# First three weight pieces in buffers of their own, shared with the general path's pool, and some instructions pinned in program order

## The chip, the cores and the metric

One core of a Trainium2 chip. The time is the device time of one execution in microseconds (us). The engines are PE (TensorE), DVE (VectorE), ACT (ScalarE), POOL (GpSimd) and SP (SyncE, which here only issues DMA transfers and register work). Three runs of the kernel before gave 1166.86, 1168.65 and 1170.96 us; the median is 1168.65.

## The reference

Three stages, each feeding the next. All data are fp32.

```python
# attention: B, H, S, D = 4, 8, 768, 64; first 4 keys (sink) and a window of 128 keys are kept
scores = where(is_sink | in_window, q @ k.T / sqrt(D), -1e9)
a = softmax(scores);  x = a @ v            # -> x: 3072 tokens x 512
# feed-forward: w_in 512 x 2048, w_out 2048 x 512
h = maximum(x @ w_in, 0);  x = (h * h) @ w_out
# top-1 mixture: 8 experts, w1 512 x 1024, w2 1024 x 512
e = argmax(x @ w_gate);  g = softmax(x @ w_gate)[e] * sigmoid((x @ w_og)[e])
out = g * (maximum(x @ w1[e], 0) @ w2[e])
```

`n_sink` and `window` are inputs. The kernel handles the values 4 and 128 on its fast path and any other on a slow general path.

## The kernel before, in words

**Tiling.** The 3072 tokens are taken as 12 blocks of 256 (`t` = 0 to 11), each with four pairs of heads (`p` = 0 to 3) and two halves of 128 queries (`n`). For a block, attention gives `xT` (128 x 4 x 256); then 16 steps `l1(t, j)` (L565, with squaring at L569 and splitting at L571 and L572) and `l2(t, j)` (L581) do the feed-forward with j over 16 slices of 128 hidden units. Attention of block t+1 is woven into the feed-forward of block t. After block 11 the mixture's slots follow.

**Precision.** fp32 matrices are split into a high and a low part, and three matmuls replace one. So the weights must be split once, before block 0 can use them: `conv(c)`, c = 0 to 31, takes one piece of 512 KB. An even c is the slice of `w_in` that `l1(0, c/2)` needs (tile `WI`); an odd c is the slice of `w_out` for `l2` (tile `WOa` for the first eight, `WOb` for the others). A conversion is a load by SP (L273 or L277) into a buffer `craw`, two ACT instructions in place (L283, L284), two DVE `SCALAR_TENSOR_TENSOR` into `fbuf` (L286, L287), a copy to the high part (L289 on ACT, or L291 on DVE for every third c), and the low part by subtraction on POOL (L292). `fbuf` has two halves in turn. `craw` shares a ring of three buffers (tag `stage`) with the scratch tiles `tmp` of `setup` and `setup2`.

**The start.** `scalars` loads the two inputs and computes `gen`. Every engine reads `gen` into a register (`values_load`, L784) and branches on it (L785): the branch holds `general`, the slow path, which isn't taken here. The pool `genp` of the slow path takes its SBUF from where the pool `wpool2` with `WOb` lies after it. Behind the branch a loop over 46 half steps places attention of block 0 (and the first events of block 1), `setup2` and one `conv` every third half step (`cstep`); then `split_x(0)` (L528 to L532) makes the `xT` of block 0, and the main loop begins. In it `cstep` brings the other conversions while block 0's feed-forward runs.

```python
def cstep(n):
    ...
        while st_["load"] < min(NC, st_["done"] + 2):   # loads run two ahead
            rests[st_["load"]] = conv(st_["load"])
```

**What sets the order.** Outside the last stage the order on each engine isn't the program's: a scheduler orders instructions by priority and by its own costs, between branches, and it may lift an instruction ahead of a branch when nothing forbids it. `tc.keep_in_program_order(x)` takes that freedom from an instruction. Engines run their lists in order. `fill` (L86) issues matmuls on a constant tile `idle` that only keep PE busy. `loads(t, p)` brings k, q, v of a pair of heads (L314) into tiles `kn`, `qn`, `vn`, two buffers each. In attention, `scores` makes the masked scores on DVE (L425, two instructions with the read of the minimum), the exponent on ACT (L428) and the normalisation (L438 on DVE, L440 on ACT); `prep_k` adds four sink keys to `kT` on POOL (L336 to L340); `setup2` has many small POOL instructions, among them the memset L230, and two DVE casts (L243) that read what it wrote.

Of the kernel before, what the change touches and what calls it, by code (L numbers as in the profile page):

```python
# [8 lines left out]
F32 = mybir.dt.float32  # L9
F32R = mybir.dt.float32r  # L10
BF16 = mybir.dt.bfloat16
I32 = mybir.dt.int32
# [23 lines left out]

SPLITS = {6: (0, 0), 8: (2, 0), 11: (0, 1), 12: (1, 0), 13: (2, 1), 14: (3, 0)}
NSLOT = NT // 128 + NE - 1
PRE = 2
# [3 lines left out]
def kern(ctx, tc, q, k, v, n_sink, window, w_in, w_out, w_gate, w_og, w1, w2, out):  # L43
# [34 lines left out]
    two = const.tile([1, 2], I32, name="two")  # L78
    idle = const.tile([128, 512], BF16, name="idle")
    V.memset(idle[:], 1.0)  # L80

    def fill(o, n):

        w = o.shape[-1]
        for _ in range(n):
            PE.matmul(o, lhsT=idle[:, 0:128], rhs=idle[:, 0:w], start=True, stop=True)  # L86

# [96 lines left out]
    def setup():  # L184
# [19 lines left out]
        A.activation(out=zz, in_=zz, func=AF.Exp)  # L204

    def setup2():

# [25 lines left out]
        wg = [tmp[:, 256:384].rearrange("p (a k c) -> p a k c", a=2, k=4)[:, n] for n in range(2)]  # L233
        SY.dma_start(out=wg[0][:, :, 0:NE], in_=w_gate.rearrange("(k p) e -> p k e", p=128))
        SY.dma_start(out=wg[0][:, :, NE:2 * NE], in_=w_og.rearrange("(k p) e -> p k e", p=128))
        G.memset(w3[:], 0.0)
# [32 lines left out]
    def conv(c):  # L269
        j, which = divmod(c, 2)  # L270
        raw = cv.tile([128, 512, 2], I32, tag="stage", bufs=3, name="craw")
        if which == 0:
# [7 lines left out]
        def rest():  # L280
            L, Hh = raw[:, :, 0], raw[:, :, 1]

            A.activation(out=Hh.bitcast(F32), in_=Hh.bitcast(F32), func=AF.Copy, scale=2.0 ** -112)  # L283
            A.activation(out=L, in_=L.bitcast(U32), func=AF.Copy, scale=0.93 * 2.0 ** -29)  # L284
# [18 lines left out]
    def loads(t, p):  # L303
        b, u = divmod(t, NQ // 2)
        s0 = 256 * u
        for nm, src, m in (("k", k, 3), ("q", q, 2), ("v", v, 3)):
            x = att.tile([128, m, 2, D], F32, tag=nm + "n", name=nm + "n", bufs=2)
            lo = s0 - 128 * (m - 2)
            o = 0
            if lo < 0:  # L310
                lo, o = 0, 1
            nb = m - o
            for e in range(2):
                (A if nm == "q" and t == 0 and p < 2 else SY).dma_start(out=x[:, o:m, e, :],  # L314
                             in_=src[b, 2 * p + e, lo:lo + 128 * nb, :].rearrange("(n s) d -> s n d", s=128))
            nat[nm, t, p] = x
        if u == 0 and p == 0:
            x = att.tile([H * NS, D], F32, tag="vs", name="vs", bufs=1)
            SY.dma_start(out=x[:], in_=v[b, :, 0:NS, :])
            nat["vs", b] = x  # L320
# [446 lines left out]
    st_ = dict(load=0, done=0)  # L767

    def cstep(n):
        for _ in range(n):  # L770
            if st_["done"] >= NC:
                return
            while st_["load"] < min(NC, st_["done"] + 2):
                rests[st_["load"]] = conv(st_["load"])
                st_["load"] += 1
            rests.pop(st_["done"])()
            st_["done"] += 1
# [7 lines left out]
    with tc.If(gv > 0):  # L785
        with tc.tile_pool(name="genp", bufs=1) as gp_:
            general(gp_)
    wpool2 = ctx.enter_context(tc.tile_pool(name="wpool2", bufs=1))
    WO[1] = wpool2.tile([128, NF // 2, 2, 512], F32R, name="WOb")
    WOf[1] = WO[1][:].rearrange("p j a f -> p (j a f)")  # L790
    events = sorted((e for t in range(NBLK) for e in attn_events(t)), key=lambda e: e[0])
# [15 lines left out]
    for h in range(-46, 0):  # L807
        run_to(h)
        if h == -38:
            setup2()  # L810
        if h >= -39 and h % 3 == 0:
            cstep(1)
    split_x(0)

# [304 lines left out]
```

## Time and profile before

| | |
|---|---|
| median of three runs | 1168.65 us |
| profiled execution, its own time | 1168.36 us |
| its span | 1166.5 us |
| PE busy, matmuls | 1127.8 us (97%) |
| DVE busy | 739.7 us (63%) |
| ACT busy | 637.1 us (55%) |
| POOL busy | 468.5 us (40%) |

The span is what the trace covers; the 1.9 us beside it lie around it. A share of busy time is an average over stages with different limits, so the stretches are looked at one by one.

### The profile page before, as it was taken

The numbers are of one execution on the slowest core, as the hardware profiler recorded it, in microseconds if no ns is written. First come the engines' busy times: TensorE is split into PE (matmuls) and PEld (weight loads), VectorE is DVE, ScalarE is ACT, GpSimd is POOL, SyncE is SP. The second block draws the span as 40 slices with busy tenths as digits, with TensorE's granted clock in tenths as the row PEclk, the third lists the DMA queues.
The fourth block names the chain that finished last, engine by engine and source line by source line (L and its number), as shares of the span: only waits on it lengthen the run. The fifth ranks groups of instructions, "written<-read, shape, count | busy, mean of one in ns | idle before, by whom it ended". The sixth has DMA issues, their size and how long they took to land. (4 is left out here: it accounts for less than half of the span.)

```text
span 1166.5 us, 23899 instructions
## 1 busy us (share of the span) xinstructions
PE 1127.8 (97%) x7082; PEld 947.2 (81%) x7082; DVE 739.7 (63%) x2018; ACT 637.1 (55%) x1750; POOL 468.5 (40%) x949
## 2 busy tenths in 40 slices
PE   7898899999999999999999999999999999999996
PEld 3565688888888888888888888997788888888884
DVE  5889866667676667676667676557412566763153
ACT  5867676767676767676776766554232232232200
POOL 4466664336565326565335655220211122221111
PEclk9989899999999999999999999999999999999998
DMA  5656411111211121111211110296411456653110
GB/s 134 185 171 187 110 28 45 38 46 38 55 30 46 30 55 37 46 42 29 52 37 47 35 48 2 28 252 156 127 38 46 152 182 215 218 201 132 46 45 23
DMA packets 139388, 100.08 MB, mean 86 GB/s; under 512 B 103904, under 2 KB 112224, under 8 KB 139235
## 3 DMA queue, kind: packets, MB, share of 16 engines
q1 hardware_dynamic: 132674, 83.85, 26.1%
q0 software_dynamic: 5472, 14.19, 3.7%
q8 instruction: 64, 1.05, 0.4%
q14 instruction: 90, 0.73, 0.2%
q10 hardware_dynamic: 1088, 0.26, 0.1%
HBM read 85.56 MB, written 13.76 MB: 85 GB/s over the span
## 5 line engine op out<-in xcount | busy, mean ns | idle before, releaser
L565 PE MATMUL psh<-xT,WI 128*128 128x256 f32 x2304 | 314.0, 284 | 11.4 <-POOL WI L292 6.3
L565 PEld LDWEIGHTS psh<-xT,WI 128*128 128x128 f32 x2304 | 294.1, 189 | 29.9 <-POOL WI L292 8.8
L887 PE MATMUL psh<-WI,xt 128*128 (+1 forms) x672 | 165.1, 399 | 1.0 <-ACT xt L867 0.7
L569 DVE TENSOR_TENSOR r<-r 128x256 f32<-128x256 f32 x184 | 86.3, 470 | 118.1 <-ACT r L568 117.3
L581 PE MATMUL psx<-WOa,h 128*128 128x512 f32 x576 | 159.8, 410 | 0.6 <-DVE h L572 0.6
L581 PE MATMUL psx<-WOb,h 128*128 128x512 f32 x576 | 157.2, 409 | 1.8 <-DVE h L572 1.2
L887 PEld LDWEIGHTS psh<-WI,xt 128*128 128x128 f32 x672 | 123.9, 188 | 29.3 <-ACT xt L867 1.4
L581 PEld LDWEIGHTS psx<-WOb,h 128*128 128x128 f32 x576 | 102.7, 191 | 22.6 <-DVE h L572 2.5
L903 DVE TENSOR_TENSOR ht<-psht,ht 128x512 fp32r<-128x512 f32 x56 | 38.5, 689 | 123.6 <-ACT ht L867 123.2
L581 PEld LDWEIGHTS psx<-WOa,h 128*128 128x128 f32 x576 | 101.6, 190 | 18.2 <-DVE h L572 0.8
L428 ACT ACTIVATE P<-P,st 128x260 f32<-128x260 f32 (+1 forms) x192 | 93.8, 489 | 34.9 <-DVE st L425 34.1
L925 POOL DMA_INDIRECT out_dram<-xg,pidx x28 | 28.7, 1026 | 198.7 <-ACT xg L924 157.2
L568 ACT ACTIVATE r<-psh 128x256 f32<-128x256 f32 x192 | 71.5, 372 | 66.9 <-PE psh L565 65.2
L572 DVE TENSOR_TENSOR h<-r,h 128x256 fp32r<-128x256 f32 x192 | 93.5, 487 | 19.0 <-ACT h L571 13.6
L473 POOL TENSOR_SCALAR_AFFINE_SELECT PT<-PT 128x256 fp32r<-128x256 f32 x224 | 98.1, 471 | 15.1 <-DVE PT L469 14.8
L571 ACT ACTIVATE h<-r 128x256 fp32r<-128x256 f32 x192 | 79.5, 414 | 34.4 <-DVE r L569 26.6
L425 DVE CUSTOM_DVE_ANT_0 P<-pss,M 128x260 f32<-128x260 f32 (+1 forms) x184 | 72.6, 402 | 22.0 <-PE pss L421 9.7
L916 PE MATMUL psy<-WOb,ht 128*128 (+1 forms) x336 | 85.0, 402 | 0.0
L916 PE MATMUL psy<-WOa,ht 128*128 (+1 forms) x336 | 84.0, 397 | 0.0
L893 ACT ACTIVATE r<-psh 128x512 f32<-128x512 f32 x48 | 28.7, 598 | 101.0 <-PE psh L887 99.1
L440 ACT ACTIVATE P<-P,st 128x132 f32<-128x132 f32 (+2 forms) x168 | 62.2, 415 | 35.3 <-DVE st L431 34.1
L508 POOL TENSOR_TENSOR xr<-tB,tC 128x128 f32<-128x128 f32 x80 | 37.7, 471 | 101.3 <-DVE tB L507 96.6
(441 smaller groups left out, 1932.2 us busy)
## 6 DMA issues: line engine op xcount, KB each, us to landing
raw<-in_moe_w_dram SPq DMA_DIRECT2D x36, 1024.0 KB, 6.0
craw<-in_moe_w_in_dram SPq DMA_DIRECT2D x16, 512.0 KB, 4.0
craw<-in_moe_w_out_dram SPq DMA_DIRECT2D x16, 512.0 KB, 3.9
x2tab<-x2s SPq DMA_DIRECT2D x24, 256.5 KB, 3.7
kn<-in_k_dram SPq DMA_DIRECT2D x64, 96.0 KB, 2.3
vn<-in_v_dram SPq DMA_DIRECT2D x64, 96.0 KB, 2.3
qn<-in_q_dram SPq DMA_DIRECT2D x92, 64.0 KB, 2.1
kn<-in_k_dram SPq DMA_DIRECT2D x32, 64.0 KB, 2.1
```

Of the source, the lines that this page charges most:

```text
L425: V.tensor_tensor_reduce(out=P[:, e, 0:W], in0=ps[e][:, 0:W], in1=mask[:, 0:W], scale=-SCALE, scalar=3.0e38, op0=ALU.add, op1=ALU.min, acc ...
L428: A.activation(out=P[:, e, 0:W], in_=P[:, e, 0:W], func=AF.Exp, scale=-1.0, bias=st[:, e:e + 1], accum_out=st[:, 4 + e:5 + e])
L440: A.activation(out=P[:, e, 0:W], in_=P[:, e, 0:W], func=AF.Copy, scale=st[:, 6 + e:7 + e])
L473: G.affine_select(out=both[:, 1 - b, e], in_=bf[:, 0, e], pattern=[[0, 2], [1 - 2 * b, 128]], compare_op=ALU.is_gt if b else ALU.is_ge, fi ...
L565: PE.matmul(ps[:], lhsT=WI[:, j, a_, kk, :], rhs=x[:, b_, kk, :], start=(n == 0), stop=(n == 11))
L568: A.activation(out=hq[:], in_=ps[:], func=AF.Relu)
L569: (G if t == 0 and j % 2 else V).tensor_tensor(out=hq[:], in0=hq[:], in1=hq[:], op=ALU.mult)
L571: A.activation(out=o[:, 0], in_=hq[:], func=AF.Copy)
L572: V.tensor_tensor(out=o[:, 1], in0=hq[:], in1=o[:, 0].bitcast(F32), op=ALU.subtract)
L581: PE.matmul(acc[t][m][:], lhsT=o[:, a_, 128 * m:128 * m + 128], rhs=WO[j // 8][:, j % 8, b_, :], start=(j == 0 and n == 0), stop=(j == NF ...
L887: PE.matmul(ps[:], lhsT=o[:, a_, kk, :], rhs=wview(n, par + 2048 * b_ + 512 * kk, 512), start=(c == 0), stop=(c == 11))
L916: PE.matmul(yp[s][:], lhsT=o[:, a_, kk, :], rhs=wview(2 + n, par + 2048 * b_ + 512 * kk, 512), start=(n == 0 and kk == 0 and c == 0), stop ...
```

## The change

The first three pieces (c = 0, 1, 2) get buffers `braw` of their own in a pool `boot`. It is opened after the pool of the general path is closed and takes the same SBUF; `wpool2` with `WOb` is opened after `boot` is closed, behind the opening loop. The three loads are asked for at once behind the branch (`fetch(NBOOT)`). The first ACT instruction of these three conversions, the two loads of the gate weights and the loads of the pair p = 2 of block 0 are kept in program order. `vn` has three buffers in place of two. `idle` is 128 x 128 in place of 128 x 512, and `fill` reads it repeatedly through a broadcast.

```diff
-    idle = const.tile([128, 512], BF16, name="idle")
+    idle = const.tile([128, 128], BF16, name="idle")
...
-            PE.matmul(o, lhsT=idle[:, 0:128], rhs=idle[:, 0:w], start=True, stop=True)
+            PE.matmul(o[:, 0:w // 128 * 128], lhsT=idle[:], rhs=idle[:, None, :].broadcast_to([128, w // 128, 128]), start=True, stop=True)
...
+    pin = tc.keep_in_program_order
...
-        SY.dma_start(out=wg[0][:, :, 0:NE], in_=w_gate.rearrange("(k p) e -> p k e", p=128))
-        SY.dma_start(out=wg[0][:, :, NE:2 * NE], in_=w_og.rearrange("(k p) e -> p k e", p=128))
+        pin(SY.dma_start(out=wg[0][:, :, 0:NE], in_=w_gate.rearrange("(k p) e -> p k e", p=128)))
+        pin(SY.dma_start(out=wg[0][:, :, NE:2 * NE], in_=w_og.rearrange("(k p) e -> p k e", p=128)))
...
-        raw = cv.tile([128, 512, 2], I32, tag="stage", bufs=3, name="craw")
+        if c < NBOOT:
+            raw = braw[c]
+        else:
+            raw = cv.tile([128, 512, 2], I32, tag="stage", bufs=3, name="craw")
...
-            A.activation(out=Hh.bitcast(F32), in_=Hh.bitcast(F32), func=AF.Copy, scale=2.0 ** -112)
+            x = A.activation(out=Hh.bitcast(F32), in_=Hh.bitcast(F32), func=AF.Copy, scale=2.0 ** -112)
+            if c < NBOOT:
+                tc.keep_in_program_order(x)
...
-            x = att.tile([128, m, 2, D], F32, tag=nm + "n", name=nm + "n", bufs=2)
+            x = att.tile([128, m, 2, D], F32, tag=nm + "n", name=nm + "n", bufs=3 if nm == "v" else 2)
...
-                (A if nm == "q" and t == 0 and p < 2 else SY).dma_start(out=x[:, o:m, e, :],
+                x_ = (A if nm == "q" and t == 0 and p < 2 else SY).dma_start(out=x[:, o:m, e, :],
...
+                if t == 0 and p == 2:
+                    pin(x_)
...
+    def fetch(n):
+        while st_["load"] < n:
+            rests[st_["load"]] = conv(st_["load"])
+            st_["load"] += 1
...
-            while st_["load"] < min(NC, st_["done"] + 2):
-                rests[st_["load"]] = conv(st_["load"])
-                st_["load"] += 1
+            fetch(min(NC, st_["done"] + 2))
...
-    wpool2 = ctx.enter_context(tc.tile_pool(name="wpool2", bufs=1))
-    WO[1] = wpool2.tile([128, NF // 2, 2, 512], F32R, name="WOb")
-    WOf[1] = WO[1][:].rearrange("p j a f -> p (j a f)")
+    bootS = ExitStack()
+    boot = bootS.enter_context(tc.tile_pool(name="boot", bufs=1))
+    braw = [boot.tile([128, 512, 2], I32, name=f"braw{n}") for n in range(NBOOT)]
+    fetch(NBOOT)
...
+    bootS.close()
+    wpool2 = ctx.enter_context(tc.tile_pool(name="wpool2", bufs=1))
+    WO[1] = wpool2.tile([128, NF // 2, 2, 512], F32R, name="WOb")
+    WOf[1] = WO[1][:].rearrange("p j a f -> p (j a f)")
     split_x(0)
```

The change also moves instructions, up to the second `split_x` (that of block 1); behind it the lists of all engines but for SP's loads of v are the same as before. Three places. The lines of the changed kernel stand up to 19 higher: its L290 and L293 are L283 and L284 before, L295 and L296 are L286 and L287, L436 is L425, L449 is L438, L543 is L532, L799 is L785.

ACT at the branch, before. `craw` is the buffer of a conversion, L784 reads `gen`, and L428 is the exponent of the first scores:

```order
L314 DMA qn<-in_q_dram 128x2x64 [waits DMAHW1_49]
L283 ACTIVATE craw<-craw 128x512 [waits DMAHW5_49]
L784 TENSOR_LOAD gen [waits DVE_49]
L785 COMPARE_AND_BRANCH
...
L284 ACTIVATE craw<-craw 128x512
L283 ACTIVATE craw<-craw 128x512 [waits DMAHW6_49]
L284 ACTIVATE craw<-craw 128x512
L428 ACTIVATE P,st<-P,st 128x128 [waits DVE_49] x2
```

and now:

```order
L323 DMA qn<-in_q_dram 128x2x64 [waits DMAHW1_49]
L798 TENSOR_LOAD gen [waits DVE_49]
L799 COMPARE_AND_BRANCH
...
L439 ACTIVATE P,st<-P,st 128x128 [waits DVE_49] x2
L439 ACTIVATE P,st<-P,st 128x260 [waits DVE_49] x2
L451 ACTIVATE P<-P,st 128x128 [waits DVE_49,Activation_49]
L376 ACTIVATE qT<-psq 128x256 [waits PE_49]
L451 ACTIVATE P<-P,st 128x260 [waits DVE_49,Activation_49]
L472 ACTIVATE PT_721<-pspt 128x256 [waits PE_49]
L290 ACTIVATE braw_595<-braw_595 128x512 [waits DMAHW4_49,DMAHW3_49,DMAHW5_49,DMAHW2_49,DMAHW6_49,DMAHW1_49,DMAHW7_49,DMAHW0_49,Pool_49]
```

Before, the first conversion stands ahead of the reading of `gen` on ACT, and so its wait for the first piece does too; now three steps of attention come first, and the conversions follow one by one.

SP at the branch, before (two pieces ahead of the branch, the loads of the pair p = 2 behind it):

```order
L784 ISA x2
L273 DMA craw<-in_moe_w_in_dram 128x4x256 [waits DMAHW5_49]
L277 DMA craw<-in_moe_w_out_dram 128x1024 [waits DMAHW6_49]
L785 COMPARE_AND_BRANCH
...
L319 DMA vs<-in_v_dram 32x1x64 [waits DMAHW7_49,DMAHW0_49,Pool_49]
L314 DMA kn<-in_k_dram 128x2x64 [waits DMAHW1_49,PE_49]
```

and now:

```order
L798 ISA x2
L799 COMPARE_AND_BRANCH
...
L280 DMA braw_595<-in_moe_w_in_dram 128x4x256 [waits DMAHW2_49,DMAHW3_49,DMAHW1_49,DMAHW4_49,DMAHW0_49,DMAHW5_49,DVE_49,DMAHW6_49,PE_49,DMAHW7_49,Activation_49,Pool_49]
L284 DMA braw_596<-in_moe_w_out_dram 128x1024
L280 DMA braw_597<-in_moe_w_in_dram 128x4x256
L323 DMA kn<-in_k_dram 128x2x64 [waits PE_49]
L323 DMA kn<-in_k_dram 128x2x64
```

The pieces moved from ahead of the branch to behind it, and the third stands with them.

DVE ahead of the first `xT` split (`split_x(0)`: L532 before, L543 now). Before:

```order
L286 SCALAR_TENSOR_TENSOR fbuf<-craw 128x512 [waits DMAHW4_49,Activation_49]
L425 ISA P,st<-pss_1237,M_111 128x260 [waits PE_49]
L425 ISA st 128x1
L287 SCALAR_TENSOR_TENSOR fbuf<-craw,fbuf 128x512 [waits DVE_49]
L286 SCALAR_TENSOR_TENSOR fbuf<-craw 128x512 [waits DMAHW5_49,Activation_49,Pool_49]
L532 TENSOR_TENSOR xT<-xr,xT 128x256 [waits DMAHW0_49,Activation_49]
```

and now:

```order
L295 SCALAR_TENSOR_TENSOR fbuf<-craw 128x512 [waits DMAHW3_49,Activation_49,Pool_49]
L345 COPY kT<-psk__1107 128x3x128 [waits PE_49,Pool_49]
L539 COMPARE_AND_BRANCH
L539 UNCONDITIONAL_BRANCH x2
L441 TENSOR_SCALAR st<-st 128x2 [waits Activation_49]
L296 SCALAR_TENSOR_TENSOR fbuf<-craw,fbuf 128x512 [waits DVE_49]
L442 RECIPROCAL st<-st 128x2 [waits DVE_49]
L543 TENSOR_TENSOR xT<-xr,xT 128x256 [waits DMAHW6_49,Activation_49]
```

Counted from the branch on `gen` to this first split, DVE's list had 13 of the conversions' `SCALAR_TENSOR_TENSOR` (seven L286, six L287), two of their casts (L291), 22 masked scores (L425, each with its read) and 12 normalisations (L438); now it has 8, 1, 20 and 10. What is missing stands behind the split.

## Rows read from the trace of the kernel before

**Rows 1.** Busy time by stretch, whole core; first row names the columns:

```profile
core 0: us, PE busy (x) PEld busy (x) DVE busy (x) ACT busy (x) POOL busy (x), PEclk, DMA share, GB/s
140.00:1166.50 1026.50, 1009.03 (x6450) 867.32 (x6448) 626.29 (x1746) 541.13 (x1511) 389.21 (x806) 1.00 0.27 75
...
15.14:49.26 34.12, 31.60 (x194) 17.89 (x193) 27.47 (x100) 28.23 (x85) 12.75 (x35) 0.98 0.63 161
49.26:139.00 89.74, 77.58 (x404) 56.84 (x404) 81.93 (x151) 63.36 (x149) 58.99 (x70) 0.91 0.58 171
...
60.50:70.50 10.00, 9.60 (x32) 6.71 (x33) 6.98 (x12) 5.22 (x12) 6.25 (x9) 0.51 0.49 139
132.00:138.50 6.50, 6.50 (x20) 4.83 (x19) 6.12 (x14) 2.96 (x7) 3.54 (x7) 0.53 0.01 1
```

**Rows 2.** Timeline of SP's issues, 7 to 14 us (start, length, instruction):

```profile
7.58 0.37 SPq L273 DMA_DIRECT2D craw<-in_moe_w_in_dram  x1
7.99 0.50 SPq L277 DMA_DIRECT2D craw<-in_moe_w_out_dram  x1
...
13.41 0.80 SPq L319 DMA_DIRECT2D vs<-in_v_dram  x1
```

**Rows 3.** Timeline of ACT, 7 to 14 us (in brackets: idle before, and releaser):

```profile
11.87 0.67 ACT L283 ACTIVATE craw<-craw 128x512 f32<-128x512 f32 x1 [7.97 <-SPq L785]
12.97 0.68 ACT L284 ACTIVATE craw<-craw 128x512 int32<-128x512 uint32 x1 [0.43 <-ACTq L785]
```

**Rows 4.** Timeline of PE, start to 14 us:

```profile
1.54 4.98 PE L86 MATMUL psi<-idle 128*128 128x512 bf16 x12 [1.54 <-DVE idle L80]
...
12.94 0.59 PE L86 MATMUL psx<-idle 128*128 128x260 bf16 x2 [3.88 <-ACTq L785]
```

**Rows 5.** Timeline of DVE, 9 to 18 us:

```profile
9.56 0.41 DVE L367 COPY qT<-psq 128x256 f32<-128x256 f32 x1
13.68 0.69 DVE L286 SCALAR_TENSOR_TENSOR fbuf<-craw 128x512 int32<-128x512 int32 x1 [3.71 <-ACT craw L284]
15.14 0.29 DVE L425 CUSTOM_DVE_ANT_0 P<-pss,M 128x128 f32<-128x128 f32 x1 [0.77 <-PE pss L417]
...
16.01 0.43 DVE L425 CUSTOM_DVE_ANT_0 P<-psx,M 128x260 f32<-128x260 f32 x1
...
17.75 0.22 DVE L243 CAST psk<-tmp 128x128 fp32r<-128x128 f32 x1
```

**Rows 6.** Timeline of POOL, 11 to 13 us:

```profile
11.21 0.18 POOL L336 CAST sk<-kT 128x4 fp32r<-128x4 f32 x1
...
11.95 0.52 POOL L230 MEMSET tmp<- 128x513 f32 x1
```

**Rows 7.** Timeline of DVE, 46 to 50 us:

```profile
46.84 0.34 DVE L438 TENSOR_SCALAR P<-P,st 128x260 f32<-128x260 f32 x1
47.11 0.68 DVE L286 SCALAR_TENSOR_TENSOR fbuf<-craw 128x512 int32<-128x512 int32 x1
47.71 0.42 DVE L425 CUSTOM_DVE_ANT_0 P<-pss,M 128x260 f32<-128x260 f32 x1
...
48.05 0.68 DVE L287 SCALAR_TENSOR_TENSOR fbuf<-craw,fbuf 128x512 int32<-128x512 int32 x1
48.66 0.68 DVE L286 SCALAR_TENSOR_TENSOR fbuf<-craw 128x512 int32<-128x512 int32 x1
49.26 0.42 DVE L532 TENSOR_TENSOR xT<-xr,xT 128x256 fp32r<-128x256 f32 x1
```

**Rows 8.** Timelines of DVE and POOL at 55.6 us:

```profile
55.61 1.81 DVE L286 SCALAR_TENSOR_TENSOR fbuf<-craw 128x512 int32<-128x512 int32 x1
...
55.58 1.30 POOL L292 TENSOR_TENSOR WOa<-fbuf,WOa 128x512 fp32r<-128x512 f32 x1 [2.03 <-DVE WOa L291]
```

**Rows 9.** Timeline of DVE at 70 us:

```profile
70.74 0.42 DVE L367 COPY qT<-psq 128x256 f32<-128x256 f32 x1 [3.22 <-PE psq L360]
```

**Rows 10.** Timeline of PE at 131 us:

```profile
131.34 1.69 PE L565 MATMUL psh<-xT,WI 128*128 128x256 f32 x10 [2.14 <-POOL WI L292]
```

More of the change, by code (lines that the diff above doesn't have):

```diff
@@ L37 @@
 SPLITS = {6: (0, 0), 8: (2, 0), 11: (0, 1), 12: (1, 0), 13: (2, 1), 14: (3, 0)}
+NBOOT = 3
 NSLOT = NT // 128 + NE - 1
```

## The prediction

> **What bounds the kernel now.** I read the busy time by stretch first. From 140 us to the end PE has 1009.03 of 1026.50 us of matmuls at the full granted clock [rows 1]: that stretch is bound by PE. The lists of the engines are unchanged there, so this change can only move the point at which the stretch begins. Ahead of it there are two others. From the first masked scores (15.14 us) to the first xT split (49.26) DVE is busy 27.47 of 34.12 us (80.5%) and ACT 28.23 (83%) [rows 1]: a chain PE, DVE, ACT, POOL in turn, with conversions between its links. From 49.26 to 139 DVE is busy 81.93 of 89.74 us, 91.3%, and no other engine has so much [rows 1], for PE's matmuls there wait for pieces of weights. The work of DVE is what has to be got through before 139 us.
>
> Then I read the timelines of each engine at the start. SP issues the first two pieces at 7.58 and 7.99, and nothing more until 13.41 [rows 2], though k and q of the third pair are still to be loaded. ACT's first conversion begins at 11.87 after 7.97 us idle, and the next ACT instruction, which stands behind the branch, at 12.97 [rows 3]. PE's next matmul waits 3.88 us for ACT's branch, until 12.94 [rows 4]. DVE ends its copy at 9.97 and has nothing until 13.68 [rows 5]. The reader sees one wait: ACT has a conversion ahead of its branch, this waits for a piece of 512 KB, and PE, DVE and SP wait for the branch's end or for that piece.
>
> **The stall at the start.** With the pieces moved behind the branch, ACT reads gen when the others do, and the 3.88 us of PE lose their releaser. POOL is late next. Its set-up runs without a gap to 12.47 us (11.95 + 0.52) [rows 6], behind the branch in both orders. Two of its results are awaited. DVE's two casts now stand ahead of the first masked scores and need the 513-wide memset; four small POOL instructions of some 0.13 us from start to start move behind it, so it ends at about 12.0. Two casts of 0.22 us [rows 5] and a copy of 0.41 bring the first mask to about 12.8, against 15.14: 2.3 us earlier. The second scores need the sink keys at the end of the set-up, 12.5, and a PE step of 0.5 to 1; their mask comes at about 13.2, against 16.01: 2.8 earlier. I take **-2.5 us**. The ends are 0 (another wait takes the place) and -3.9 (all of PE's wait). The casts themselves leave the stretch after: 0.44 x 0.8 = **-0.3**.
>
> **Conversions that move back.** The order shows 13 of the conversions' two-input steps ahead of the first split before, and 8 now; one of the 13 ran at 13.68, in the stall, so the stretch from 15.14 loses four, and the stretch after 49.26 gains five. From start to start such a step takes 0.61 us (48.05 to 48.66 to 49.26), a masked score with its read 0.34 (47.71 to 48.05), a normalisation 0.27 (46.84 to 47.11) [rows 7]; the cast I price like a mask. The first stretch is rid of 4 x 0.61 + 0.34 + 2 x 0.34 + 2 x 0.27 = 4.0 us of DVE. It is a chain in which DVE is busy 80.5%, so I let that share come off: **-3.2**. The ends are 0, where the chain never waited for a conversion, and -4.0. The second stretch gets 5 x 0.61 + 0.34 + 0.68 + 0.54 = 4.6 us more, and as DVE is busy 91.3% there nearly all lengthens it: **+4.2**, between +3.7 (were the share only the 80.5% of the first stretch) and +4.6.
>
> Not in this sum: a conversion's step that meets POOL's subtraction. At 55.61 it took 1.81 us in place of 0.68, while POOL's 1.30 us ran from 55.58 [rows 8], 1.13 us more. The Trainium skill, page "SBUF — State Buffer", section "Who interferes with whom", says that a DVE instruction with two inputs from SBUF and a GpSimd instruction that reads SBUF exclude each other, and that the later one waits for the whole of the other. The row agrees. By that rule alone each displaced conversion would add up to 1.13 us in the busy stretch and the sum would come out at +1.6 in place of -1.8; I keep it as part of a rival, since such meetings occur in the first stretch too.
>
> **Edits that I price at nothing.** The third piece comes well ahead of its use now, but ACT had no wait for it that would go; if its place ahead of k and q of the third pair holds these up, they have until the chain of the first two pairs is through. The fourth piece stands later in SP's list, behind loads that wait for PE; ACT's use of it is later too. If the cover fails, ACT waits once for a landing, about as long as 7.58 to 11.87, 4.3 us [rows 2, 3]. The third vn buffer only moves loads that come early. The smaller memset stands ahead of a wait of DVE for the inputs. The broadcast in fill reads as many columns; twelve fills take 4.98 us [rows 4] and would have to double (+5.0) to reach past the branch. I know no reason for it, and give that end little weight.
>
> **Sum.** -2.5 - 0.3 - 3.2 + 4.2 = -1.8 us. Against the profiled execution's own 1168.36 that is 1166.6; the median of the runs is 0.3 higher, within their spread.
>
> **Rivals.**
> *Faster: a spell at the half clock is not there.* From 60.5 to 70.5 us PE had the lower level, 1.2 GHz (0.51 granted), and again from 132 to 138.5 (0.53) [rows 1]; before the second, PE had waited 2.14 us for a weight piece [rows 10]. In the first spell DVE waited 3.22 us for a transpose behind slow matmuls [rows 9]. With the order in this stretch changed, the spell may fall elsewhere or be missing: -1.8 - 3.2 = -5.0, **1163.4**. For it: the waits that precede it hang on single conversions. Against it: conversions are further back, so PE starves at the same place.
> *Slower: the backlog of conversions.* The attention of block 0 was bound by its own links, so the first stretch doesn't shorten, and three displaced conversions each meet POOL's subtraction in the busy stretch: -2.8 + 4.2 + 3 x 1.13 = +4.8, **1173.2**. It decides when the first stretch gives back less than 1.3 us of the 4.0. For it: the busy share of DVE there is no proof of queueing. Against it: ACT, at 83%, loses conversions as well.
> *Nothing comes of it.* The change doesn't do what its buffers promise: the pieces are issued later than 7.58, since they wait behind the branch, and the conversions of the first pieces end when they did. The gain of the start is given back one to one: 0 to +1, **1168.7**.
>
> **How the numbers follow.** Forecast (-4 to 0): 0.47. Faster rival: 0.27. Slower: 0.14. Nothing: 0.12. About 0.3% (3.5 us) is what a measurement of this kernel can tell from no change. Faster by more: the faster rival but for a little, and the lower edge of the forecast, 0.26 + 0.08 = 0.34. Slower by more: the slower rival and a failed cover, 0.15. Within: 0.51. The range goes to the other side of both rivals' half: 1161.0 to 1172.0, which leaves out some 0.1 at each end; the likeliest case alone is 1164.4 to 1168.4.
>
> **What would show it.** Right: ACT's branch at about 7.4 us; no wait of PE for it; the first mask at 12.5 to 13; the first xT split at 42 to 45 us in place of 49.26; DVE over 90% busy from there to about 137; the rest of the trace as before. Wrong: a first split later than 46 (the chain was not held by conversions), more than twelve steps over 1.5 us among the conversions behind it (meetings with POOL), an ACT wait for a landing, or a different count and place of half-clock spells. If the stretch from the second split to the end differs from before by over 2 us, the ground of this argument, that only the opening moves, is wrong.

## The result, and the profile after

Six runs of the changed kernel gave 1173.05 to 1177.07 us, median 1175.44; six of the kernel before on the same occasion 1165.42 to 1170.96, median 1167.42. The ratio is 1.0066, 95% interval 1.0051 to 1.0080: slower by some 8 us, where 1.8 us less was forecast. The profiled execution took 1177.07 us, its span is 1175.0. The experiments show that the size differs from occasion to occasion (1.0048 and 1.0043 later), together with the time that TensorE spends at its half clock; the sign doesn't.

The start came out as forecast. Timeline of the changed kernel, SP, ACT, POOL, PE and DVE in turn:

```profile
9.12 0.38 SPq L280 DMA_DIRECT2D braw<-in_moe_w_in_dram  x1
...
12.67 0.40 ACT L439 ACTIVATE P<-P,st 128x128 f32<-128x128 f32 x1 [9.28 <-DVE st L436]
...
11.13 0.52 POOL L234 MEMSET tmp<- 128x513 f32 x1
...
12.74 0.71 PE L428 MATMUL psx<-kT,qT 64*128 64x260 f32 x4 [2.07 <-POOL kT L351]
...
11.69 0.42 DVE L247 CAST psk<-tmp 128x128 fp32r<-128x128 f32 x2 [1.69 <-POOL tmp L234]
...
12.35 0.27 DVE L436 CUSTOM_DVE_ANT_0 P<-pss,M 128x128 f32<-128x128 f32 x1
...
13.48 0.43 DVE L436 CUSTOM_DVE_ANT_0 P<-psx,M 128x260 f32<-128x260 f32 x1 [0.64 <-PE psx L428]
```

No engine waits for ACT's branch any more [rows 3, 4]; POOL is late next, as its 513-wide memset and the sink keys hold DVE's casts and PE's second scores. The first mask is at 12.35 against 15.14, the second pair at 13.48 against 16.01 [rows 5].

All of it is gone by the first xT split. Busy time by stretch, changed kernel (columns as in rows 1): from the first mask to that split, the part of it at the half clock, from there to the second split, and the rest:

```profile
12.35:49.44 37.09, 35.42 (x173) 19.04 (x173) 21.52 (x88) 25.57 (x79) 8.11 (x31) 0.77 0.49 123
14.05:31.11 17.06, 16.96 (x58) 8.45 (x57) 7.19 (x31) 10.16 (x31) 1.85 (x5) 0.50 0.40 101
49.44:148.99 99.55, 84.66 (x435) 59.71 (x436) 86.65 (x162) 70.64 (x164) 63.52 (x77) 0.91 0.58 172
148.99:1175.00 1026.01, 1009.23 (x6445) 867.23 (x6443) 627.12 (x1748) 540.04 (x1508) 383.96 (x806) 1.00 0.27 75
```

and the kernel before, the last two of these stretches, cut at its own second split (140.06 us):

```profile
49.26:140.06 90.80, 78.64 (x411) 57.86 (x411) 81.94 (x152) 63.81 (x151) 58.99 (x70) 0.91 0.58 169
140.06:1166.50 1026.44, 1008.97 (x6449) 867.26 (x6448) 626.28 (x1746) 541.07 (x1510) 389.21 (x806) 1.00 0.27 75
```

The last stretch is unchanged (1026.0 and 1026.4 us). The first is 37.09 us long in place of 34.12, although DVE and ACT have less to do in it: PE is granted 1.2 GHz from 14.05 to 31.11 us and is busy 16.96 of these 17.06 us. The second is 99.55 us in place of 90.80: 4.71 more of DVE's work, and 4.04 more in which DVE is idle (12.90 in place of 8.86). The longest waits of DVE there, changed kernel (what waited, releaser: us in total, times, longest):

```profile
DVE P L436 <- PE pss L432: 3.7, 1, 3.7
DVE P L436 <- PE pss L428: 3.0, 2, 2.2
DVE r L580 <- ACT r L579: 2.3, 1, 2.3
```

and before, where the one long wait is that of rows 9:

```profile
DVE qT L367 <- PE psq L360: 3.2, 1, 3.2
```

The first of the three, in the timeline of the changed kernel (POOL, PE, DVE, ACT):

```profile
119.05 0.20 POOL L456 TENSOR_TENSOR psk<-P,psk 128x8 fp32r<-128x8 f32 x1
...
119.31 0.47 PE L526 MATMUL psst<-ident,psk 128*128 128x128 f32 x1 [0.70 <-POOL psk L456]
...
120.76 0.80 PE L432 MATMUL pss<-kT,qT 64*128 64x260 f32 x2
...
121.49 2.00 PE L592 MATMUL psx<-WOb,h 128*128 128x512 f32 x4
...
123.42 0.63 PE L432 MATMUL pss<-kT,qT 64*128 64x260 f32 x4
...
124.09 0.43 DVE L436 CUSTOM_DVE_ANT_0 P<-pss,M 128x260 f32<-128x260 f32 x1 [3.72 <-PE pss L432]
...
125.17 0.64 ACT L298 ACTIVATE WI<-fbuf 128x512 fp32r<-128x512 f32 x1 [4.02 <-DVE fbuf L296]
```

A masked score of block 1 now stands on DVE's list between the two steps of the 25th conversion, where none stood before. PE has its scores late: ahead of them it waits 0.70 us for POOL's sink work and does 2.00 us of feed-forward matmuls (L592), most of them in a half-clock spell (116.45 to 123.27). The conversion waits with the mask, and ACT's copy of the converted piece waits 4.02 us in turn. The same wait is in the later traces of the changed kernel, described below: 3.8 us in e13, where a half-clock spell also runs into it (until 116.95), and 2.0 in e12 and in e17, where none does. It isn't in those of e2 and e18, which have two vn buffers.

**The yardstick.** A better one than the first split is the end of the 32nd and last conversion, POOL's last subtraction from `fbuf`, and ahead of it the issue of the fifth piece's load. Timeline of SP and POOL, before:

```profile
33.54 0.41 SPq L273 DMA_DIRECT2D craw<-in_moe_w_in_dram  x1
...
141.69 1.28 POOL L292 TENSOR_TENSOR WOb<-fbuf,WOb 128x512 fp32r<-128x512 f32 x1
```

and the changed kernel:

```profile
45.19 0.41 SPq L280 DMA_DIRECT2D craw<-in_moe_w_in_dram  x1
...
150.51 1.53 POOL L301 TENSOR_TENSOR WOb<-fbuf,WOb 128x512 fp32r<-128x512 f32 x1
```

From that end (143.0 and 152.0 us) to the end of the span it is 1023.5 us before and 1023.0 after. In eighteen of the twenty traces it is 1022.5 to 1025.3; the two others are named below.

### The profile page after: what moved, and what is told of

Its sections match the earlier page's. It is cut to its first block, busy times and chain, and to the rows that moved or that the text cites. A ratio compares the mean times of both kernels' runs of the same rounds, so it can differ in the third digit from the quotient of the medians.

```text
span 1175.0 us, 23909 instructions
## 1 busy us (share of the span) xinstructions
PE 1136.0 (97%) x7082; PEld 949.2 (81%) x7082; DVE 739.0 (63%) x2018; ACT 637.7 (54%) x1750; POOL 463.0 (39%) x949
## 5 line engine op out<-in xcount | busy, mean ns | idle before, releaser
L576 PE MATMUL psh<-xT,WI 128*128 128x256 f32 x2304 | 314.9, 285 | 12.5 <-POOL WI L301 8.8
L592 PE MATMUL psx<-WOb,h 128*128 128x512 f32 x576 | 159.4, 411 | 1.3 <-ACT h L582 0.9
L592 PE MATMUL psx<-WOa,h 128*128 128x512 f32 x576 | 158.6, 409 | 0.7 <-ACT h L582 0.7
L906 PEld LDWEIGHTS psh<-WI,xt 128*128 128x128 f32 x672 | 124.0, 188 | 29.2 <-ACT xt L886 1.4
L592 PEld LDWEIGHTS psx<-WOb,h 128*128 128x128 f32 x576 | 102.6, 191 | 23.3 <-ACT h L582 2.7
L592 PEld LDWEIGHTS psx<-WOa,h 128*128 128x128 f32 x576 | 100.9, 189 | 19.5 <-issue 1.0
L583 DVE TENSOR_TENSOR h<-r,h 128x256 fp32r<-128x256 f32 x192 | 90.1, 469 | 18.1 <-ACT h L582 12.7
L436 DVE CUSTOM_DVE_ANT_0 P<-pss,M 128x260 f32<-128x260 f32 (+1 forms) x184 | 72.7, 402 | 27.7 <-PE pss L432 13.3
```

The source lines that it names most:

```text
L436: V.tensor_tensor_reduce(out=P[:, e, 0:W], in0=ps[e][:, 0:W], in1=mask[:, 0:W], scale=-SCALE, scalar=3.0e38, op0=ALU.add, op1=ALU.min, acc ...
L576: PE.matmul(ps[:], lhsT=WI[:, j, a_, kk, :], rhs=x[:, b_, kk, :], start=(n == 0), stop=(n == 11))
L583: V.tensor_tensor(out=o[:, 1], in0=hq[:], in1=o[:, 0].bitcast(F32), op=ALU.subtract)
L592: PE.matmul(acc[t][m][:], lhsT=o[:, a_, 128 * m:128 * m + 128], rhs=WO[j // 8][:, j % 8, b_, :], start=(j == 0 and n == 0), stop=(j == NF ...
L906: PE.matmul(ps[:], lhsT=o[:, a_, kk, :], rhs=wview(n, par + 2048 * b_ + 512 * kk, 512), start=(c == 0), stop=(c == 11))
```

## The experiments

"Half-clock time" of an execution is 2 x (1 - its mean granted clock) x its span, that is the time at 1.2 GHz; as the clock is on record to 0.001, it comes in steps of some 2.3 us. In every trace 6 to 9.5 us of it lie at the very end. `c7` and `c32` are the times at which the seventh and the 32nd conversion were done in the profiled run. Ratios are to the kernel before on the same occasion. The occasions ran on different chips (e1 to e4, e5 to e8, e9 to e12, e13 to e16, and e17 with e18 on one each), so the chip is a rival for whatever differs between occasions, not for what differs within one.

### The fill, and the third vn buffer

The first suspect was the new fill, since PE is busy with fills in the long spell. The plain fill needs more room than is left, so the third vn buffer goes with it, and a control has that alone.

```diff
# e1_plain_fill: idle 128x512 and the plain rhs again, and
# e2_two_vn: this alone
-            ... bufs=3 if nm == "v" else 2)
+            ... bufs=2)
# e3_before_bcast: the kernel before with
-    idle = const.tile([128, 512], BF16, name="idle")
+    idle = const.tile([128, 128], BF16, name="idle")
+            PE.matmul(o[:, 0:w // 128 * 128], lhsT=idle[:], rhs=idle[:, None, :].broadcast_to([128, w // 128, 128]), ...)
# e4_four_narrow: the changed kernel with
+            for j in range(w // 128):
+                PE.matmul(o[:, 128 * j:128 * j + 128], lhsT=idle[:], rhs=idle[:], start=True, stop=True)
```

e1: 

> The changed kernel with its fill matmuls as before (rhs a plain 128x512 tile, no broadcast) and two vn buffers instead of three, which pays for the larger tile. Theory F (the broadcast fill lets TensorE's clock stay at its lower level from 14.05 to 31.11 us, and the slow matmuls there undo the earlier start): half clock between 10 and 35 us for at most 3.5 us, first xT split at 42 to 46 us in place of 49.44, time 1164 to 1169 us. Theory O (the new order leaves PE idle just before 14 us, so the clock falls and stays down whatever the fill reads): the spell of about 17 us is there again, first split at 48 to 51, time 1173 to 1177. Theory B (the clock is a side matter; the conversions moved back make the second stretch longer): first split early, but the second split still at 147 or later, time 1172 to 1177.

e2: 

> The changed kernel with two vn buffers instead of three, nothing else: the control of the run with the plain fill. All of the theories expect the changed kernel's time, 1173 to 1177 us, and its half-clock spell from about 14 to 31 us. If the third buffer has a part in it, the time is off that by over 2 us.

e3: 

> The kernel before, with only the fill of the change: a 128x128 tile read four times by a broadcast. Theory F: the half-clock spell that begins near 13 us lasts over 6 us in place of 3.4, the first split is at 52 to 58 us in place of 49.26, time 1171 to 1178 us. Theories O and B: as before, 1165 to 1169 us, spell 3.4 us, first split near 49.

e4: 

> The changed kernel with each fill of 512 columns written as four matmuls of 128 plain columns (the same 128x128 tile, no broadcast): as many columns, the same space. Theory F in the form that the broadcast's way of reading is at fault: as the run with the plain fill, spell at most 3.5 us, 1164 to 1169 us. Theory F in the form that any re-reading of one small tile is at fault, and theory O: the long spell stays, 1173 to 1178 us.

| run | us | ratio (95%) | c7 | c32 |
|---|---|---|---|---|
| e1 plain fill, two vn | 1165.60 | 0.9999 (0.9984 to 1.0015) | 54.5 | 141.2 |
| e2 two vn | 1165.82 | 1.0004 (0.9992 to 1.0015) | 55.2 | 139.8 |
| e3 before, broadcast fill | 1165.25 | 0.9994 (0.9983 to 1.0005) | 53.7 | 139.9 |
| e4 four narrow fills | 1175.39 | 1.0077 (1.0060 to 1.0094) | 61.2 | 148.3 |

The fill has no part: e2 has it and is rid of the loss, e3 has it and shows nothing. (e4 also changes the lists, as it has more instructions; with three vn buffers it is as slow as the change, though its trace has no long spell at the start: the half clock is there from 8.15 to 14.98 us and not again until 52.53. So its time came as forecast, the spell didn't, and the loss doesn't need that spell.) All three theories had given e2 the changed kernel's time, and all three were wrong: what had been a mere control took the whole loss away, and without it e1 would have passed for a proof of theory F. The third vn buffer, which holds nothing that is needed early, is what counts when the boot buffers and the pins are there too; what it does alone, e5 asks below.

### What the third buffer does

Without a third buffer, a load of v stands on SP's list behind the wait for the buffer of two pairs earlier; with it, the scheduler puts v of a pair ahead of the k and q that follow, and the loads of a whole pair ahead of the fifth piece. The fifth piece's load in e2 and last conversion (the changed kernel: 45.19 above):

```profile
32.25 0.38 SPq L280 DMA_DIRECT2D craw<-in_moe_w_in_dram  x1
...
138.56 1.28 POOL L301 TENSOR_TENSOR WOb<-fbuf,WOb 128x512 fp32r<-128x512 f32 x1
```

and in a second trace of the changed kernel, one without a long spell at the start (e12, below):

```profile
39.38 0.41 SPq L280 DMA_DIRECT2D craw<-in_moe_w_in_dram  x1
...
142.34 1.53 POOL L301 TENSOR_TENSOR WOb<-fbuf,WOb 128x512 fp32r<-128x512 f32 x1
```

So 7.1 us of the load's delay come of the lists and the other 5.8 of the spell. DVE's list has 10 two-input steps ahead of the first split in e1 and e2, and 8 in the change, against 13 before. Four kernels part the buffer itself (theory V) from the place of the conversions in the lists (theory L):

```diff
# e5_before_third_vn: e3 with
-            ... bufs=2)
+            ... bufs=3 if nm == "v" else 2)
# e6_loads_not_pinned: e2 without
-                if t == 0 and p == 2:
-                    pin(x_)
# e7_no_early_conversions: e2 with NBOOT = 0 and
-        if h >= -39 and h % 3 == 0:
+        if False:
# e8_third_vn_no_boot: the changed kernel with
-NBOOT = 3
+NBOOT = 0
```

e5: 

> The kernel before with the fill of the change (measured alone as no change; it makes room) and a third vn buffer; no boot buffers, no pins. DVE's list still has 13 two-input conversion steps ahead of the first xT split. Theory V (the third vn buffer itself costs some 9 us, by what it moves on SP's and POOL's lists): 1172 to 1177 us, second split at 145 or later. Theory L (what costs is that conversions stand later in the lists; the third buffer matters only where it pushes them back): 1164 to 1169 us, 32nd conversion done at 138 to 143 us as in the kernel before.

e6: 

> The changed kernel with two vn buffers, and without the program order on k and q of the third pair. DVE's list has 8 two-input conversion steps ahead of the first split, as in the changed kernel, against 10 with that order and two vn buffers. Theory L: 1171 to 1177 us, the sixth conversion done at 56 us or later, the 32nd at 146 or later. Theory V: as the two-buffer control, 1164 to 1168 us.

e7: 

> The changed kernel with two vn buffers, no boot buffers and no conversion step asked for ahead of the block's first split; 8 two-input steps still stand there because the lists let them slip forward, none among the first eight masked scores. What it tells of the first stretch: if the chain of block 0's attention is held by conversions (my price of -0.8 us per us taken out), the first split comes 4 to 6 us after... earlier than in the two-buffer control relative to the first mask, 27 to 29 us from mask to split; if the chain is bound by its own links, 31 to 33 us as in the control (32.7). Theory L: the 32nd conversion at 146 us or later, 1172 to 1180 us. Theory V: 1164 to 1169 us.

e8: 

> The changed kernel with its third vn buffer but no boot buffers (the pieces are fetched as before). DVE's list has 10 two-input steps ahead of the first split, against 13 before and 8 in the change. Theory L: between the two, 1167 to 1172 us. Theory V: 1173 to 1177 us. If the boot buffers themselves are what hurts: 1164 to 1168 us.

| run | two-input steps ahead | us | ratio (95%) | c7 | c32 |
|---|---|---|---|---|---|
| e5 | 13 | 1168.87 | 1.0003 (0.9984 to 1.0021) | 57.4 | 142.6 |
| e6 | 8 | 1171.95 | 1.0029 (1.0015 to 1.0043) | 58.5 | 144.8 |
| e7 | 8, late among them | 1178.21 | 1.0084 (1.0049 to 1.0119) | 65.4 | 151.9 |
| e8 | 10 | 1168.47 | 1.0002 (0.9990 to 1.0015) | 55.4 | 140.1 |

The times come as theory L has them, and those of V don't: with a third buffer and 13 or 10 steps ahead the ratio shows no loss; with two buffers and 8 ahead it does. Two signs beside the times missed. In e6 the sixth conversion was done at 53.5 us and the 32nd at 144.8, earlier than L's 56 and 146. In e7 it is 42.9 us from the first mask to the first split, longer than either of the two cases (27 to 29, 31 to 33), with 10.2 us of it at the half clock; so e7 doesn't tell what holds the first stretch. It does show that the first split is no yardstick: in e5 it came at 53.18, 3.9 us later than before, in a spell from 12.6 to 26.2 us, and cost nothing that the ratio tells; in e8 it came at 45.46, 3.8 earlier, and gained nothing. What both share with the kernel before is `c32`.

### More of the conversions early, and a faster cast

```diff
# e9_change_conv_first (60), e10_conv_much_first (200): the changed kernel with
-            cstep(1)
+            with tc.high_priority(60):
+                cstep(1)
# e11_casts_on_act: e2 with
-            if c % 3 != 1:
+            if True:
# e16_two_vn_earlier: e2 with
-        if h >= -39 and h % 3 == 0:
+        if h >= -45 and h % 3 == 0:
```

e9: 

> The changed kernel with everything in it, the third vn buffer and the boot buffers too, but the conversions asked for ahead of the first split get a raised priority, so that 15 two-input steps (8 in the change, 13 before) stand ahead of the first split in DVE's list. Theory L (the end follows the conversions: in every run so far the span is the time of the 32nd conversion plus 1023 to 1025 us, and the last 25 take 3.4 to 3.6 us each): seventh conversion done at 50 to 54 us, 32nd at 136 to 141, 1160 to 1166 us. Any theory in which the third vn buffer, the boot buffers or the pins cost by themselves: 1170 us or more.

e10: 

> The same with a higher priority: 30 two-input steps ahead of the first split. Theory L: fifteen conversions are done by the first split, which itself comes late, at 55 to 65 us; 32nd conversion at 130 to 138, 1155 to 1162 us, if attention and conversions only share engines. If the attention of block 0 bounds the opening as well (it then starts the expert matmuls of the block too late), 1165 to 1175 us.

e11: 

> The two-buffer control with all casts of the conversions on ACT (11 of them leave DVE, some 0.4 us each, and cost ACT some 0.6). If DVE's busy time sets the rate of the conversions (91% in the second stretch): 3.45 us per conversion becomes about 3.3, 32nd at 135 to 138 us, 1160 to 1164 us. If a chain through ACT, DVE and POOL sets it: no faster, 1164 to 1170 us.

e16: 

> The two-buffer control with conversions asked for from the sixth step earlier on: 12 two-input steps ahead of the first split against 10. Theory L: two steps and what they carry, 1 to 2 us earlier: 1163 to 1166 us. Theory K expects that too, at the same half-clock time.

| run | us | ratio (95%) | first split | c7 | c32 | half-clock time, median |
|---|---|---|---|---|---|---|
| e9 | 1178.64 | 1.0118 (1.0095 to 1.0140) | 52.09 | 53.7 | 142.5 | 47.1 |
| e10 | 1179.43 | 1.0113 (1.0090 to 1.0135) | 74.42 | 47.2 | 137.1 | 58.9 |
| e11 | 1169.41 | 1.0032 (1.0018 to 1.0046) | 45.56 | 57.8 | 143.7 | 30.4 |
| e16 | 1169.95 | 1.0033 (1.0022 to 1.0043) | 50.10 | 55.5 | 144.4 | 30.4 |

None came out as theory L had it; as a rule that more conversions ahead are always better it falls. e10 has the earliest last conversion of all, 137.1, and yet a span of 1174.7: 1037.6 us behind it, one of the two exceptions. Its first split is 25 us late, and the feed-forward can't catch up. So both chains have to be ready, and the kernel before stands near the balance. e9 says more: its five runs took 1167.40 us at a mean clock of 0.993 and 1177.70 to 1183.06 at 0.978 to 0.983. The same lists gave 1167 and 1183. (The trace, and with it `c7` and `c32` in the table, is that of the 1167.40 run.) By its median e9 is what was forecast for buffers or pins that cost by themselves, 1170 or more; its run at 0.993 is still some 3 us above the kernel before at that clock (1164.44 on the same chip). So e9 doesn't exclude such a cost. e11 takes 11 casts from DVE and gains nothing per conversion (3.44 us from `c7` to `c32` against 3.39 in e2), as its second case had it, though with 20.5 us at the half clock in its second stretch against 3.4. DVE is idle for 22.3 us of that stretch there and for 8.1 in e2, so DVE's busy time alone is not what sets that pace. e16 failed as a test: the fourth piece's first ACT step isn't pinned, and it slipped ahead of the branch, so PE waited 4.17 us for ACT's branch as before and the first mask was at 15.43. That shows the start stall in one more kernel.

### The half clock

What remains is why one program took 1173 to 1177 us on one occasion and less on others. Theory K: the half-clock time differs from run to run, and the total with it.

```diff
# e12_change_again, e13_change_five, e17_change_side: the changed kernel as it is
# e18_two_vn_side: e2 as it is
# e14_change_warm (changed kernel) and e15_two_vn_warm (e2), in l1:
+        if t == 0:
+            fill(ps[:], 6)
```

e12: 

> The changed kernel once more, for a second trace of it. If the half-clock spell from 14.05 to 31.11 us is what made its first conversions late, a run with another pattern of spells has its seventh conversion done at 56 to 60 us (64.0 in the first trace) and is 4 us shorter; if the order of the lists alone does it, the seventh is done at 60 us or later whatever the spells are, and the span is again the 32nd conversion plus 1023 to 1025 us.

e13: 

> The changed kernel once more, for the spread of its runs. Theory K (clock: the lists cost some 5 us, and the rest comes of half-clock time, which differs from run to run): runs at a mean clock of 0.99 or more at 1167 to 1170 us, runs at 0.985 or less at 1173 to 1178, on one line of about 0.27 us per us of half clock. Theory L alone (lists only): all runs at 1173 to 1178 us whatever the clock.

e14: 

> The changed kernel with six fill matmuls of 256 columns ahead of each of the first block's sixteen first-layer steps, where PE waits for weights; the lists ahead of the first split are the same. Theory K: PE's idle time there is filled, the spells at 96, 116 and 140 us go, half-clock time falls by 10 to 17 us, and the time by 3 to 5 us against the changed kernel of the same call. If the spells there cost nothing (PE waits anyway): no faster, and the fills' own time, some 0.7 us per step where PE is late, adds up to 5 us.

e15: 

> The two-buffer control with the same fills. Theory K: its half-clock time is 20 us in the median, some 9 of it at the tail; 1162 to 1165 us. If the fills get in the way: 1166 to 1170.

e17: 

> The changed kernel beside its two-buffer control, on one chip. Both causes together (lists and half-clock time): 1168 to 1176 us, on the line of its earlier runs, 1168.4 at 14 us of half clock plus some 0.26 us for each further us.

e18: 

> The two-buffer control beside the changed kernel, on one chip. If the third buffer's rearrangement of the lists costs: 1164 to 1167 us, 3 us or more under the changed kernel also at equal half-clock time. If the difference of the earlier calls was the chips': within 2 us of the changed kernel.

| run | us | ratio (95%) | half-clock time, median | c7 | c32 |
|---|---|---|---|---|---|
| the change, first occasion | 1175.44 | 1.0066 (1.0051 to 1.0080) | 36.4 | 64.0 | 152.0 |
| e12, one run | 1168.43 | | 14.0 | 58.1 | 143.9 |
| e13 | 1170.41 | 1.0048 (1.0033 to 1.0063) | 25.7 | 57.4 | 145.6 |
| e17 | 1171.02 | 1.0043 (1.0027 to 1.0058) | 29.2 | 58.3 | 143.9 |
| e18, beside e17 | 1166.17 | 1.0007 (0.9992 to 1.0023) | 19.8 | 54.6 | 139.6 |
| e14, beside e13 | 1173.85 | 1.0056 (1.0036 to 1.0076) | 21.1 | 56.4 | 149.9 |
| e15 | 1181.94 | 1.0138 (1.0121 to 1.0156) | 30.7 | 55.9 | 147.0 |

e12 is the same program as the first trace, with the lower clock for 6.8 us in place of 34.1 before 160 us. Its stretches (columns as in rows 1):

```profile
12.31:43.63 31.32, 29.68 (x173) 16.80 (x173) 21.60 (x87) 25.15 (x79) 8.15 (x31) 0.95 0.57 146
14.05:31.11 17.06, 16.98 (x98) 9.76 (x97) 11.01 (x45) 14.25 (x44) 3.98 (x12) 0.92 0.49 122
43.63:140.82 97.19, 79.78 (x435) 55.98 (x436) 87.73 (x162) 70.43 (x164) 63.72 (x77) 0.98 0.60 176
140.82:1166.40 1025.58, 1008.64 (x6445) 866.75 (x6443) 627.63 (x1748) 540.20 (x1508) 387.33 (x806) 1.00 0.26 75
```

In the same 17.06 us PE does 98 matmuls and is busy 16.98; in the first trace it does 58 and is busy 16.96. In each it has hardly a gap (a small one wouldn't show, as the ends of matmuls are modelled), in one at the lower clock for the first 2.6 us and in the other for all of them. One fill and one ACT wait show what that does to the chain. First trace:

```profile
23.39 0.63 PE L88 MATMUL psk__784<-idle 128*128 128x512 bf16 x1
...
27.16 0.28 ACT L504 ACTIVATE xr<-psh 128x128 f32<-128x128 f32 x1 [3.84 <-PE psh L502]
```

and e12:

```profile
20.55 0.38 PE L88 MATMUL psk__784<-idle 128*128 128x512 bf16 x1
...
22.79 0.28 ACT L504 ACTIVATE xr<-psh 128x128 f32<-128x128 f32 x1 [1.42 <-PE psh L502]
```

The Trainium skill, page "TensorE: Matmul & The Clock Gate", section "What's actually happening", says that sustained matmul activity releases the throttle. e12 agrees (back at 16.7 us); the first trace doesn't as far as its rows tell, where matmuls with hardly a gap from 14 us on brought the clock back only at 31.1.

Theory K holds as to the line. Taken within each kernel, the time rises with the half-clock time, over 234 executions by 0.26 us per us (correlation 0.77); for example e18 takes 1164.64 us at a mean clock of 0.993 and 1173.74 at 0.981. Moved along this slope to one half-clock time of 15 us, the kernel before is at 1163.9, e18 and e2 at 1164.9, e13 and e17 at 1167.5 and 1167.7, the first occasion at 1170.0. Side by side, e17 and e18 differ by 4.85 us, and by 2.8 on that reckoning, just under the 3 that was forecast: the third vn buffer's lists cost that at an equal clock, and the rest goes with PE's longer time at the lower clock. This is a reckoning along a line and no test: whether the clock makes the time or late work makes both isn't parted by any run here.

The reckoning also changes how e5 to e8 read. The kernel before is at 1165.3 on their chip; e5 is 0.9 above it, e8 2.5 and e6 3.8, against 3.8 and 3.9 for e13 and e17 above theirs, and 1.2 and 1.1 for e2 and e18. e8 owes its ratio of 1.0002 in part to a short half-clock time (18.7 us in the median, 25.7 for the kernel before). So a third buffer alone costs little, and the whole loss needs the boot buffers beside it; how much of it each makes at an equal clock stays open.

e14 and e15 failed to lower the time. In e14 the fills took 4.6 us of half-clock time away, but the last conversion is at 149.9; in e15 there are 1032.9 us from the last conversion to the end, the other exception; that the fills stand ahead of matmuls that are late by then is a likely reason, which no run tests. That a warm PE would win the 3 to 5 us back is so far not shown.

None of the versions beats the kernel before by more than the measurement tells; e3, the nearest, is at 0.9994 (0.9983 to 1.0005).

## Why the prediction was wrong

**The start stall, -2.5: right.** -2.79 at the first mask, -2.53 at the second pair. e16, in which a conversion slipped back ahead of the branch, has the stall again.

**First stretch, -3.5 with the casts: right in size, but not safe.** From the first mask to the first split it is 31.32 us in e12 and 30.60 in e13, against 34.12: -2.8 and -3.5. Some luck is in this. DVE's busy time there fell by 5.9 us (27.47 to 21.60) and not by the 4.4 of the sum, which was counted from start to start; so 0.5 to 0.6 of it came off in place of 0.8. The first split at 42.9 to 43.8 in three of the four traces, too, lies in the forecast 42 to 45. In the profiled run the 17 us at the half clock made it 37.09, +3.0. The prediction had half-clock spells as a gain only (the faster rival, a spell that is missing); that the new order could bring a longer one, in a stretch in which fills keep PE busy, has no price in any of its cases, though "a different count and place of half-clock spells" stands among its signs of being wrong.

**Second stretch, +4.2: the step that failed.** Measured: +8.75 in the first trace, and 99.58 us, +8.8, in e13, both with the 17 us of half clock that the stretch had before. DVE's work grew by 4.71, as the 4.6 of the sum has it. The other 4.04 are waits of DVE. The 91% busy share was a fair price for the added work, but the sum took it that DVE would not wait more than before, and the new order puts masked scores, which hang on PE and POOL, ahead of conversion steps.

**Edits at nothing: the third vn buffer was the wrong one.** "The third vn buffer only moves loads that come early" was the sentence. What it moved them past is the pieces' loads: the fifth is issued at 39.38 in place of 32.25. e18 beside e17: 4.85 us. The second stretch shows where that lies. In turn the kernel before with the new fill (e3, on another chip than the other two), the changed kernel (e17) and the changed kernel with two vn buffers (e18), each with 6.8 us of half clock in it (columns as in rows 1):

```profile
49.38:137.45 88.07, 75.30 (x416) 55.05 (x416) 82.41 (x152) 64.40 (x152) 58.58 (x70) 0.96 0.60 176
43.83:140.87 97.04, 81.12 (x435) 57.07 (x436) 87.69 (x162) 70.55 (x164) 63.79 (x77) 0.96 0.60 176
44.44:136.73 92.29, 79.27 (x432) 57.39 (x431) 84.98 (x162) 67.71 (x157) 63.48 (x76) 0.96 0.59 173
```

The longest waits of DVE in e17's stretch are two of those in the first trace, the second of them 2.0 us in place of 3.7, as no half-clock spell runs into it:

```profile
DVE r L580 <- ACT r L579: 2.2, 1, 2.2
DVE P L436 <- PE pss L432: 2.0, 1, 2.0
```

In e18 neither is there. So the stretch is 9.0 us longer with three vn buffers and 4.2 with two. That the last figure is the forecast's is luck: three steps moved behind the split in e18, not five, and DVE's work grew by 2.6. Nor did the rest of the sum come in without the third buffer: e18's start is 2.85 us earlier than e3's and its first stretch 2.1 shorter, so that 0.7 is left at the second split, and e2 and e18 are no faster than the kernel before (1.0004 and 1.0007). The broadcast fill, which was given a small chance of +5.0, costs nothing (e3). The fourth piece's cover held: ACT begins it without a wait for a landing.

**The profiled run added up.** Start -2.8, first stretch +3.0, second +8.75: the second split is 8.9 us late (148.99 against 140.06), and as the rest takes 0.4 less, the span is 8.5 longer. The forecast for the second split was 138.3; of the 10.7 us between, 6.5 belong to the first stretch, that is the spell, and 4.6 to the second, less 0.3 at the start.

**The rivals.** The slower one came nearest in number (1173.2), with the wrong mechanism. Its added collisions didn't come: seven conversion steps took over 1.5 us in the second stretch against nine before, and the time beyond 0.68 us in the steps over 1 us fell from 12.5 to 10.8 us, so such collisions had no part in the loss. (The Trainium skill's rule on them, page "SBUF — State Buffer", section "Who interferes with whom", is not contradicted by that; it was only not what cost here.) Its first half, that the first stretch doesn't shorten, is refuted by e12 and e13. The rival that nothing comes of it had the first piece issued late, at 9.12, and this is so, but not its price. "More than 2 us between the second split and the end" did not occur.

## What to carry to other kernels

Where a fixed series of pieces has to be through before the rest can run at full rate, read its progress, the time of the n-th piece, as the yardstick; here the span was that of the last piece plus 1024 us, while a milestone 5 us early gained nothing. A buffer more for one stream isn't free under a scheduler: ask which loads it lets pass in the same queue, and which waits land ahead of the work that bounds. Before a difference of some us is put down to an edit, compare on one chip and at an equal granted clock.

## What was not expected of the hardware

The same program, with PE busy for 16.96 and 16.98 of the same 17.06 us, ran them at 1.2 GHz in one execution and mostly at 2.4 in another; a run's time at the lower clock varied from 14 to 42 us for the changed kernel and from 14 to 37 for the kernel before, at 0.26 us of the total per us. Why the first occasion had more of it (36.4 us in the median against 25.7 and 29.2 later) is open; the chip is one candidate.
